# A retention layer and two expert layers on one core: 136 DMAs issued by GpSimd in place of SyncE

## The chip, the cores and the metric

The kernel runs on one core of one Trainium2 chip. A core has a matrix engine (TensorE, PE in the profile), a vector engine (VectorE, DVE), a scalar engine (ScalarE, ACT), a general engine (GpSimd, POOL), and a fifth engine, SyncE (SP), that computes nothing and issues transfers. Each engine works through its own instructions in order and waits for others on semaphores. A transfer (DMA) is an instruction of the engine that issues it: SP, ACT or POOL. The bytes are then moved by 16 DMA engines that the core shares out among all of them. An instruction behind a DMA issue that waits has to wait too, whatever it needs itself.

The metric is the time of one execution in microseconds (us). Lower is better.

## What is computed

```python
def _attn_ref(q, k, v):                                  # B, H, S, D = 4, 8, 576, 64
    scores = scale * np.matmul(q, k.transpose(0, 1, 3, 2))
    Dmat = np.where(rel >= 0, gamma[:, None, None] ** rel[None, :, :], 0.0)
    return np.matmul(scores * Dmat[None, :, :, :], v)
def _moe_ref(x, w_in, w_out):                            # 2304 x 512, 512 x 2048, 2048 x 512
    h = x @ w_in
    g = np.where(h > 0.0, h, alpha * (np.exp(np.minimum(h, 0.0)) - 1.0))
    return g @ w_out
def _moe2_ref(x, w_in, w_out):
    h = np.maximum(x @ w_in, 0.0)
    return h * h @ w_out
def reference(**kwargs):
    attn_out = _attn_ref(**attn_kwargs)
    x = np.ascontiguousarray(attn_out.transpose(0, 2, 1, 3)).reshape(B * S, H * D)
    x = _moe_ref(x=x, **moe_kwargs)
    return _moe2_ref(x=x, **moe2_kwargs)
```

Attention with a decaying mask gives 2304 tokens of width 512. Two expert layers follow: 512 to 2048 and back, the first with an exponential unit between its products, the second with a squared rectifier. The weights arrive as 64-bit floats and are turned into fp32 on the chip.

## The kernel before, in words

Every fp32 product is three matmuls of a faster type: `split` (L157 to L160) cuts an operand into a high part (ACT, L159) and the rest (DVE, L160), and `mm3` (L162 to L165) runs high by high, high by low, low by high. Products, splits and what lies between them are the whole of the work, with PE the busiest engine.

**Attention and layer one.** The 2304 tokens come in five blocks of 512, 512, 256, 512 and 512. For each block the attention runs in chunks of tokens (the q, k and v of a chunk are loaded at L256 and scaled at L267, transposed at L293, scores at L306, outputs at L321 and L325, the running state at L335 and L341). Then for each of the 16 slices f of the hidden width the kernel computes `h` (an up product over a block, lines 163 to 165), the exponential unit (ACT L365 to L367, DVE L369 and L370), and `down(blk, f)`, which adds to four PSUM accumulators `acc0` to `acc3`. Blocks 0 and 1 are shared: they go through the slices in three groups (0 to 5, 6 to 10, 11 to 15), because their accumulators are given up in between. At the end of a group `down` parks the sums in DRAM (`parts`, L406). At the end of the next group it loads them (L394) and adds them on DVE (L402), which also sets the accumulator free. After the last slice of a block the sum is layer two's input. It is stored to the DRAM tiles `x2s0` to `x2s8` in pieces of 128 x 128 (64 KB each, L411): 16 stores for a block of 512, 8 for the block of 256, 72 in all. The tiles `x2` that hold these sums are taken from the pool `raw`, three buffers that also hold raw weights and, later, layer two's inputs `r`.

**Layer two's weights** are prepared beside this. `load_raw` (L187, L192) fetches a 64-bit slice, `to_f32` (ACT L204, L205; DVE L206 to L211) turns it into fp32 in the tile `f`, of which there are three, and `park_w` (L215) stores it in the DRAM tile `w2s`: 32 stores of 256 KB. `fetch_w` (L221) reads it back later.

**Layer two** runs as a scheme of seven products for a 2 x 2 block product, products A, B and D at L492 in 128 x 384 tiles, each of six matmuls. `inputs(u)` loads `r` from `x2s[u]` (L429; 512 KB) and makes from it the operands `T` by splits (L439: ACT L159, DVE L160) and differences (L443). u runs from 0 to 8, and u = 6, 7, 8 are the third column c = 2, which need blocks 3 and 4. The sums of products become `go` (DVE L519, L522) and are stored to `g2s` (L525). The second product of layer two is at L675.

**What sets the order.** The program is written for a scheduler that decides, for each engine, the order of its instructions by modelled times; the engine of a DMA is named in the code. So a DMA on another engine moves not only itself: the rows around it may be put in another order on every engine. Before, SP issues nearly all transfers, ACT ten, and POOL none: POOL does eight scalings at the start (L267) and otherwise nothing.

The change touches `park_w` (L214, L215) and `down` (L374 to L413). Three lines of `inputs` show what has to wait for the last of the stores:

```python
def load():
    r = raw_p.tile([P, 4, 2, P], F32, tag="raw", name="r")
    nc.sync.dma_start(out=r, in_=x2s[u])
```

Of the kernel before, what the change touches and what calls it, by code (L numbers as in the profile page):

```python
# [21 lines left out]
NF = DFF // P  # L22
# [104 lines left out]
def tile_kernel(ctx: ExitStack, tc, q, k, v, w_in1, w_out1, w_in2, w_out2, cst, out):  # L127
    nc = tc.nc
# [15 lines left out]
    parts = dram.tile([2, P, KC, TB], F32, tag="parts", name="parts")  # L144
    w2s = dram.tile([2 * NF, P, DM], F32, tag="w2s", name="w2s")
# [16 lines left out]
    def mm3(ps, l_hi, l_lo, r_hi, r_lo, first, last):  # L162
        nc.tensor.matmul(ps, l_hi, r_hi, start=first, stop=False)  # L163
        nc.tensor.matmul(ps, l_hi, r_lo, start=False, stop=False)  # L164
        nc.tensor.matmul(ps, l_lo, r_hi, start=False, stop=last)  # L165


    raws, f32s, w_t = {}, {}, {}
# [43 lines left out]
        f32s[u] = a  # L212

    def park_w(u):  # L214
        nc.sync.dma_start(out=w2s[u[1] * NF + u[2]], in_=f32s.pop(u))  # L215

    def fetch_w(u, spare=None):
        a = a_p.tile([P, NP, P], F32, tag=spare, name="f") if spare else f_p.tile([P, DM], F32, tag="f", name="f")
# [155 lines left out]
    def down(blk, f):  # L374
        n = BLOCKS[blk][1]
        g, w = g_t.pop((blk, f)), w_t[0, 1, f]
        shared = blk < 2
        first, last = (any(f == r[e] - (e == 1) for r in (GROUPS if shared else ((0, NF),))) for e in range(2))
        if first:
            acc_t[blk] = [ps_acc.tile([P, TB], F32, tag="acc", name=f"acc{m}") for m in range(KC)]  # L380

        back = shared and last and f >= GROUPS[0][1]
        end = last and f == NF - 1
        part = []
        for m in range(KC if last else 0):
            if end:
                if m % 2 == 0:
                    both = raw_p.tile([P, 2, TB], F32, tag="raw", name="x2")
                t = both[:, m % 2]
            else:  # L390
                t = n_p.tile([P, TB], F32, tag="qkv"[m % 3], name="part")
            part.append(t[:, :n])
            if back:
                nc.sync.dma_start(out=part[m], in_=parts[blk, :, m, :n])  # L394
        for m in range(KC):
            c = slice(m * P, (m + 1) * P)
            a = acc_t[blk][m][:, :n]
            mm3(a, w[:, 0, c], w[:, 1, c], g[:, 0, :n], g[:, 1, :n], first, last)
            if not last:
                continue  # L400
            if back:
                nc.vector.tensor_tensor(out=part[m], in0=a, in1=part[m], op=ALU.add)  # L402
            else:
                nc.scalar.copy(part[m], a)
            if not end:
                nc.sync.dma_start(out=parts[blk, :, m, :n], in_=part[m])  # L406
                continue
            for half in range(2):
                for j in range(n // 2 // P):
                    o = half * n // 2 + j * P  # L410
                    nc.sync.dma_start(  # L411
                        out=x2s[COL0[blk] // P + j][:, m // 2 * 2 + half, m % 2], in_=part[m][:, o:o + P]
                    )  # L413

# [382 lines left out]
    for i, (blk, f) in enumerate(ORDER1):  # L797
        def mid():
            if i == SPREAD[2][0] - 4:
                load_next(True)  # L800
                load_next(True)
                scale_next()
            for of, (lo, hi) in SPREAD.items():
                if lo <= i < hi:
                    need = 3 * len(blocks[of])
                    for _ in range((i - lo + 1) * need // (hi - lo) - (i - lo) * need // (hi - lo)):
                        attn_step()
            if at["split"] < len(w1):
                w1_to(units1(i))
            elif i >= SHARED and at["f322"] < min(len(w2), units2(i)):  # L810

                step("park", at["f322"], w2, park_w)
                with tc.issue_after(mark[0]):
                    step("f322", at["raw2"], w2, to_f32)
                while at["raw2"] < min(len(w2), at["f322"] + 2):
                    step("raw2", 99, w2, lambda u: load_raw(*u))
            if at["f322"] == len(w2):
                step("park", 99, w2, park_w)
            j = i - (len(ORDER1) - NF)

            with tc.issue_after(mark[0]):
                if j == 6:
                    run(factors(0))
                if 7 <= j < NF and j not in (10, 14):
                    next_inputs()
# [3 lines left out]
        if len(pend) > LAG:  # L829
            down(*pend.pop(0))  # L830
# [25 lines left out]
    for i, (f, c) in enumerate(seq):  # L856
        now = up2(f, c)
        for n, (at_, _) in enumerate(tasks):
            if at_ == i:
                if i in (5, 18):  # L860
                    queue.extend([lambda: None] * 2)
                queue.append(lambda n=n: expand(n))
        for k in TURNS.get(i, (1, 5, 7, 2, 6, 4, 3)):
            whose = last if k in (7, 4) else now
            if whose:
                whose[k]()
            if k in (7, 4) and pend:
                down(*pend.pop(0))
            between()
        last = now  # L870

        for g in {20: (0,), 21: (1, 2), 22: (3,), 23: (4,)}.get(i, ()):
            load_last(g)
# [33 lines left out]
```

## Time and profile before

| | us |
|---|---|
| median of three runs | 889.0 (888.3 to 893.39) |
| profiled execution, its own time | 890.2 |
| span of the profiled execution | 888.4 |
| PE busy in the span | 858.9 |
| DVE busy | 685.8 |
| ACT busy | 491.9 |
| POOL busy | 8.6 |

The span is the time from the first to the last instruction that the profile holds; 1.8 us of the profiled execution's own time lie outside it. All times below that place an event (such as 526.75) are microseconds from the start of the span. PE's granted clock was 0.99 over the span, so nothing below turns on the clock. PE is busy for 97% of the span, and the rest is spread over a few stretches. What can be won or lost by transfers is therefore read from the single places where PE stands idle and from what ends each of these waits.

### The profile page before, as it was taken

The numbers are of one execution on the slowest core, as the hardware profiler recorded it, in microseconds if no ns is written. First come the engines' busy times: TensorE is split into PE (matmuls) and PEld (weight loads), VectorE is DVE, ScalarE is ACT, GpSimd is POOL, SyncE is SP. The second block draws the span as 40 slices with busy tenths as digits, with TensorE's granted clock in tenths as the row PEclk, the third lists the DMA queues.
The fourth block names the chain that finished last, engine by engine and source line by source line (L and its number), as shares of the span: only waits on it lengthen the run. The fifth ranks groups of instructions, "written<-read, shape, count | busy, mean of one in ns | idle before, by whom it ended". The sixth has DMA issues, their size and how long they took to land.

```text
span 888.4 us, 14958 instructions
## 1 busy us (share of the span) xinstructions
PE 858.9 (97%) x5630; PEld 773.1 (87%) x5630; DVE 685.8 (77%) x1391; ACT 491.9 (55%) x961; POOL 8.6 (1%) x12
## 2 busy tenths in 40 slices
PE   7798999999998999999999999999999989999998
PEld 5676888888888988888888899999989989999997
DVE  4998888885667867766779867889874769898984
ACT  3674778673464666556767754555543434444441
POOL 3000000000000000000000000000000000000000
PEclk9999899999999999999999999999999999999999
DMA  9945306383528656534362044599997993544331
GB/s 223 269 117 160 87 33 190 119 213 96 142 60 233 173 156 184 171 107 146 129 230 89 24 126 154 161 325 349 344 324 242 402 346 132 157 141 154 120 131 37
DMA packets 157608, 155.33 MB, mean 175 GB/s; under 512 B 62816, under 2 KB 121312, under 8 KB 157536
## 3 DMA queue, kind: packets, MB, share of 16 engines
q1 hardware_dynamic: 150208, 139.69, 52.0%
q10 hardware_dynamic: 7328, 14.68, 4.6%
q8 instruction: 44, 0.72, 0.4%
q14 instruction: 28, 0.23, 0.1%
HBM read 98.77 MB, written 55.57 MB: 174 GB/s over the span
## 4 chain that ended last, share of the span: by engine, by line
PE 83%; DVE 6%; DMA 5%; issue 2%; ACT 2%; SPq 1%; ACTq 0%; DVEq 0%
PE m L675 18%; PE A L492 10%; PE acc L163 7%; PE acc L164 7%; PE h L163 7%; PE acc L165 7%; PE h L164 7%; PE h L165 7%; PE D L492 5%; PE B L492 2%; PE ps_o L325 2%; PE ps_o L321 1%; PE ps_s L306 1%; DMA q<-in_q_dram 1%; DMA g<-g2s 1%
## 5 line engine op out<-in xcount | busy, mean ns | idle before, releaser
L675 PE MATMUL m<-wo,S 128*128 128x256 f32 x1512 | 184.0, 285 | 3.6 <-ACT S L159 3.6
L675 PEld LDWEIGHTS m<-wo,S 128*128 128x128 f32 x1512 | 183.3, 193 | 4.1 <-ACT S L159 4.0
L159 ACT CAST S<-g 128x512 fp32r<-128x512 f32 (+1 forms) x144 | 75.0, 567 | 95.0 <-DVE g L659 45.9
L163 PE MATMUL h<-x,w 128*128 128x512 f32 (+1 forms) x320 | 120.4, 378 | 2.2 <-DVE t L370 1.3
L164 PE MATMUL h<-x,w 128*128 128x512 f32 (+1 forms) x320 | 118.9, 372 | 0.0
L165 PE MATMUL h<-x,w 128*128 128x512 f32 (+1 forms) x320 | 118.9, 371 | 0.0
L164 PE MATMUL acc<-g,w 128*128 128x512 f32 (+1 forms) x320 | 118.5, 371 | 0.0
L165 PE MATMUL acc<-g,w 128*128 128x512 f32 (+1 forms) x320 | 117.5, 370 | 0.0
L492 PE MATMUL A<-T,pair 128*128 128x384 f32 x576 | 114.2, 339 | 1.6 <-DVE go L519 0.8
L163 PE MATMUL acc<-g,w 128*128 128x512 f32 (+1 forms) x320 | 111.4, 375 | 2.3 <-DVE x L402 1.3
L492 PEld LDWEIGHTS A<-T,pair 128*128 128x128 f32 x576 | 102.0, 190 | 3.4 <-DVE go L519 1.6
L160 DVE TENSOR_TENSOR S<-g,S 128x512 fp32r<-128x512 f32 (+1 forms) x144 | 85.9, 623 | 23.2 <-ACT S L159 21.7
L365 ACT ACTIVATE t<-h 128x512 f32<-128x512 f32 (+1 forms) x80 | 44.5, 556 | 80.5 <-PE h L165 76.9
L369 DVE SCALAR_TENSOR_TENSOR t<-e,t 128x512 f32<-128x512 f32 (+1 forms) x80 | 50.9, 636 | 46.7 <-ACT t L367 46.5
L163 PEld LDWEIGHTS h<-x,w 128*128 128x128 f32 x320 | 60.7, 190 | 14.1 <-DVE t L370 1.8
L159 ACT CAST g<-t 128x512 fp32r<-128x512 f32 (+1 forms) x80 | 46.4, 580 | 46.5 <-DVE t L370 44.7
L163 PEld LDWEIGHTS acc<-g,w 128*128 128x128 f32 x320 | 59.4, 188 | 13.4 <-DVE x L402 1.6
L165 PEld LDWEIGHTS h<-x,w 128*128 128x128 f32 x320 | 60.8, 190 | 10.7 <-DVE w L160 0.2
L164 PEld LDWEIGHTS h<-x,w 128*128 128x128 f32 x320 | 60.9, 190 | 10.2
L164 PEld LDWEIGHTS acc<-g,w 128*128 128x128 f32 x320 | 60.3, 188 | 10.2
L165 PEld LDWEIGHTS acc<-g,w 128*128 128x128 f32 x320 | 60.2, 188 | 10.1
L492 PE MATMUL D<-T,pair 128*128 128x384 f32 x288 | 58.5, 336 | 1.9 <-ACT pair L159 0.6
(88 smaller groups left out, 1282.4 us busy)
## 6 DMA issues: line engine op xcount, KB each, us to landing
g2s<-go SPq DMA_DIRECT2D x48, 384.0 KB, 4.5
g<-g2s SPq DMA_DIRECT2D x36, 512.0 KB, 3.9
raw<-in_moe_w_in_dram SPq DMA_DIRECT2D x32, 512.0 KB, 5.8
raw<-in_moe_w_out_dram SPq DMA_DIRECT2D x32, 512.0 KB, 4.8
wo2s<-wo SPq DMA_DIRECT2D x56, 256.0 KB, 4.2
wo<-wo2s ACTq DMA_DIRECT2D x9, 1536.0 KB, 14.7
w2s<-f SPq DMA_DIRECT2D x32, 256.0 KB, 2.3
f<-w2s SPq DMA_DIRECT2D x32, 256.0 KB, 4.0
```

Of the source, the lines that this page charges most:

```text
L159: nc.scalar.copy(pair_hi, src)
L160: eng.tensor_tensor(out=pair_lo, in0=src, in1=pair_hi.bitcast(F32), op=ALU.subtract)
L163: nc.tensor.matmul(ps, l_hi, r_hi, start=first, stop=False)
L164: nc.tensor.matmul(ps, l_hi, r_lo, start=False, stop=False)
L165: nc.tensor.matmul(ps, l_lo, r_hi, start=False, stop=last)
L306: nc.tensor.matmul(ps[e][:n, p, :n], kT[r, p, :n], qT[r, p, :n], start=True, stop=True)
L321: i = nc.tensor.matmul(ps[:, p, :n], st[:, p, :], qT[:, p, :n], start=p == 0, stop=True, skip_group_check=True)
L325: nc.tensor.matmul(ps[e * D:(e + 1) * D, p, :n], vn[:n, 2 * p + e, :], live[e][:n, p, :n], start=not s, stop=True, skip_group_check=True,)
L365: nc.scalar.activation(t, h, AF.Relu, scale=-1.0)
L369: nc.vector.scalar_tensor_tensor(out=t, in0=e, scalar=1.0, in1=t, op0=ALU.add, op1=ALU.mult)
L492: ins = nc.tensor.matmul(ps, w[:, l, o:o + P], t[:, r, j], start=first and i + j == 0, stop=i + j == 3, skip_group_check=True)
L675: ins = nc.tensor.matmul(m(u, k), l[:, x], w[:, y], start=first and k in (1, 6, 4, 5), stop=j == HF - 1 and i == 2, skip_group_check=True,)
```

## The change

Four lines name another engine. What is transferred, from where to where, and how it is cut, stays the same.

```diff
     def park_w(u):
-        nc.sync.dma_start(out=w2s[u[1] * NF + u[2]], in_=f32s.pop(u))
+        nc.gpsimd.dma_start(out=w2s[u[1] * NF + u[2]], in_=f32s.pop(u))
...
             if back:
-                nc.sync.dma_start(out=part[m], in_=parts[blk, :, m, :n])
+                nc.gpsimd.dma_start(out=part[m], in_=parts[blk, :, m, :n])
...
             if not end:
-                nc.sync.dma_start(out=parts[blk, :, m, :n], in_=part[m])
+                nc.gpsimd.dma_start(out=parts[blk, :, m, :n], in_=part[m])
                 continue
...
-                    nc.sync.dma_start(
+                    nc.gpsimd.dma_start(
                         out=x2s[COL0[blk] // P + j][:, m // 2 * 2 + half, m % 2], in_=part[m][:, o:o + P]
                     )
```

That is 32 stores of L215, 16 loads of L394, 16 stores of L406 and 72 stores of L411: 136 transfers that POOL issues in place of SP.

Three places show how the instructions move. A row is a line, an operation, and its tiles as out<-in with the buffer number behind the name.

SP at the start of layer two (`x2_5141` is the last half of the last block's sums; `r_5185` and `r_5296` are the inputs u = 7 and u = 8). Before:

```order
L411 DMA x2s7_102<-x2_5141 128x128
L411 DMA x2s8_103<-x2_5141 128x128
L525 DMA g2s0_104<-go_5125 128x3x256
L429 DMA r_5185<-x2s7_102 128x1024
L429 DMA r_5296<-x2s8_103 128x1024
L221 DMA f_5581<-w2s_94 128x512
L525 DMA g2s0_104<-go_5215 128x3x256
```

Of the change:

```order
L429 DMA r_5037<-x2s6_101 128x1024
L221 DMA f_5583<-w2s_94 128x512
L221 DMA f_5581<-w2s_94 128x512
L525 DMA g2s0_104<-go_5125 128x3x256
L525 DMA g2s0_104<-go_5215 128x3x256
L525 DMA g2s1_105<-go_5227 128x3x256
L525 DMA g2s1_105<-go_5293 128x3x256
L429 DMA r_5185<-x2s7_102 128x1024
L525 DMA g2s0_104<-go_5305 128x3x256
L429 DMA r_5296<-x2s8_103 128x1024
```

The stores are gone to POOL, where they are the last 16 rows. The load of `r_5185` now stands behind three more stores of `go`, the last of them `go_5293`.

DVE at the same place, where `T7` is the first operand made from `r_5185`. Before:

```order
L522 SCALAR_TENSOR_TENSOR go_5227<-go_5227 128x3x128
L160 TENSOR_TENSOR T7_5039<-r_5185,T7_5039 128x2x128
L519 TENSOR_TENSOR go_5293<-A_5187,m5_5205 128x3x128
L160 TENSOR_TENSOR T7_5039<-r_5185,T7_5039 128x2x128
L443 TENSOR_TENSOR r_5185<-r_5185 128x256
L160 TENSOR_TENSOR T8_5044<-r_5185,T8_5044 128x2x128
L522 SCALAR_TENSOR_TENSOR go_5293<-go_5293 128x3x128
L519 TENSOR_TENSOR go_5305<-B_5298,c1_5272 128x3x128
```

Of the change:

```order
L519 TENSOR_TENSOR go_5293<-A_5187,m5_5205 128x3x128
L522 SCALAR_TENSOR_TENSOR go_5293<-go_5293 128x3x128
L519 TENSOR_TENSOR go_5305<-B_5298,c1_5272 128x3x128
L522 SCALAR_TENSOR_TENSOR go_5305<-go_5305 128x3x128
L519 TENSOR_TENSOR go_5305<-D_5276,u2_5316 128x3x128
L522 SCALAR_TENSOR_TENSOR go_5305<-go_5305 128x3x128
L519 TENSOR_TENSOR go_5371<-A_5265,m5_5283 128x3x128
L522 SCALAR_TENSOR_TENSOR go_5371<-go_5371 128x3x128
L519 TENSOR_TENSOR go_5383<-B_5376,c1_5350 128x3x128
L160 TENSOR_TENSOR T7_5039<-r_5185,T7_5039 128x2x128
L522 SCALAR_TENSOR_TENSOR go_5383<-go_5383 128x3x128
L160 TENSOR_TENSOR T7_5039<-r_5185,T7_5039 128x2x128
```

The first `T7` stands nine rows later: the sums `go_5293`, `go_5305`, `go_5371` and the first piece of `go_5383` go ahead of it.

PE at the end of the last group of block 1 (`acc2_2522` is an accumulator that DVE has to empty at L402, with the parked sum `x2_2420`, before PE may write to it again). The difference, with + for rows that the change puts there:

```order
 L165 MATMUL h_2723<-x_2019,w3_706 128x256
+L163 MATMUL h_2723<-x_2019,w3_706 128x256
...
+L321 MATMUL ps_o_2665<-qT_2560,st_109 128x128 x4
+L325 MATMUL ps_o_2665<-P0_2624,v_2262 64x128
...
+L335 MATMUL ps_u_2680<-v_2262,k_2260 64x64 x8
+L163 MATMUL h_2782<-x_2019,w4_922 128x256
...
+L293 MATMUL ps_t_2742<-cs_108,q_2500 128x128 x4
+L293 MATMUL ps_t_2749<-cs_108,k_2502 128x128 x4
 L163 MATMUL acc2_2522<-g_2329,w0_210 128x256
```

The rest of one `h` product (3 matmuls), the attention outputs `ps_o` (4 and 8), the state `ps_u` (8), a whole `h` product (12) and eight transposes now come before the first write to `acc2_2522`; before, they came behind it.

## Rows read from the trace of the kernel before

**Rows 1.** The page, section 1: engines, busy us (share of the span), instructions

```profile
PE 858.9 (97%) x5630; PEld 773.1 (87%) x5630; DVE 685.8 (77%) x1391; ACT 491.9 (55%) x961; POOL 8.6 (1%) x12
```

**Rows 2.** Stretches of 50 us: length, busy us of each engine, granted clock, DMA

```profile
150.00:200.00 50.00, 50.00 (x235) 41.13 (x235) 42.09 (x75) 35.92 (x63) 0.00 (x0) 1.00 0.60 163
...
250.00:300.00 50.00, 46.93 (x444) 43.83 (x444) 36.52 (x78) 27.26 (x62) 0.00 (x0) 1.00 0.66 174
300.00:350.00 50.00, 49.57 (x393) 43.03 (x392) 38.59 (x80) 32.63 (x69) 0.00 (x0) 1.00 0.54 149
...
500.00:550.00 50.00, 48.53 (x255) 44.73 (x254) 36.46 (x85) 27.08 (x63) 0.00 (x0) 1.00 0.35 108
550.00:600.00 50.00, 49.67 (x287) 49.33 (x286) 39.90 (x85) 27.90 (x58) 0.00 (x0) 1.00 0.72 234
```

**Rows 3.** Timeline of PE, 262 to 283: start, us, what, [idle before <-releaser]

```profile
270.74 0.39 PE L163 MATMUL acc<-g,w 128*128 128x256 f32 x1 [1.26 <-DVE x L402]
...
280.40 0.66 PE L293 MATMUL ps_t<-cs,q 128*128 128x128 f32 x4 [1.19 <-DVE x L160]
```

**Rows 4.** Timeline of SP's DMA issues, 225 to 300: start, us, what, how many

```profile
260.33 4.05 SPq L411 DMA_DIRECT2D x2s<-x  x8
...
270.71 4.91 SPq L411 DMA_DIRECT2D x2s<-x  x8
```

**Rows 5.** Chain of work that ended last, 255 to 283: start, us, what

```profile
265.69 1.85 DMA x<-parts
...
269.99 0.70 DVE x L402
...
271.12 0.12 PE acc L164
...
273.40 0.89 PE ps_o L321 x8
...
275.73 3.30 DMA q<-in_q_dram
```

**Rows 6.** Transfers: what, issuer, count, KB each, median us from issue to landing

```profile
x<-parts SPq DMA_DIRECT2D x8, 256.0 KB, 3.8
```

**Rows 7.** Chain of work that ended last, 515 to 548

```profile
525.06 1.67 DMA x2s<-x
...
526.75 4.86 DMA r<-x2s
...
532.07 0.43 DVE T L160
```

**Rows 8.** Timeline of SP's DMA issues, 500 to 560

```profile
517.60 8.37 SPq L411 DMA_DIRECT2D x2s<-x  x16
```

**Rows 9.** Timeline of PE, 530 to 566

```profile
533.02 1.32 PE L492 MATMUL A<-T,pair 128*128 128x384 f32 x6 [0.44 <-DVE go L519]
...
538.34 1.20 PE L492 MATMUL B<-T,pair 128*128 128x384 f32 x6
...
540.98 1.32 PE L492 MATMUL A<-T,pair 128*128 128x384 f32 x6 [0.39 <-DVE go L519]
...
544.23 0.34 PE L492 MATMUL D<-T,pair 128*128 128x384 f32 x1
545.21 1.15 PE L492 MATMUL D<-T,pair 128*128 128x384 f32 x5 [0.64 <-DVE T L160]
```

**Rows 10.** Timeline of DVE, 530 to 546

```profile
538.69 1.43 DVE L160 TENSOR_TENSOR T<-r,T 128x256 fp32r<-128x256 f32 x4
540.03 0.42 DVE L443 TENSOR_TENSOR r<-r 128x256 f32<-128x256 f32 x1
```

**Rows 11.** Line 411's instructions on SP: duration ns min/median/max, first and last start

```profile
L411 SPq DMA_DIRECT2D x2s<-x x72: 319/430/1814, 226.5 to 525.5; - x72
```

**Rows 12.** Groups of POOL's instructions: busy us, mean ns of one, idle before

```profile
L267 POOL TENSOR_TENSOR spare<-spare,cs 128x512 f32<-128x512 f32 x6 | 6.3, 1049 | 8.7 <-DMA spare<-in_q_dram 7.0 <-DMA spare<-in_k_dram 1.5
```

**Rows 13.** Line 206's instructions: duration ns min/median/max, first and last start

```profile
L206 DVE TENSOR_SCALAR f<-f x64: 409/420/828, 14.3 to 455.3; 128x512 f32<-128x512 f32 x64
```

## The prediction

> **What bounds the kernel now.** The page's section on engines comes first: PE is busy for 97% of the span, POOL for 1% [rows 1]. A PE that is nearly full can win little, so the next view is the table of busy time in stretches of 50 us, which says where the missing 3% lies. In the stretches that the change touches PE is full for 50.00 of 50 us where the parks and the partial sums of the first two groups are moved (150 to 200), and it loses 3.07 us in 250 to 300, 0.43 in 300 to 350, 1.47 in 500 to 550 and 0.33 in 550 to 600 [rows 2]. These 5.3 us are all that a better order of transfers could give back there. PE's own timeline then gives each idle place with what ended it: 1.26 us at 270.74 for the addition of a parked sum, 1.19 at 280.40 for a split of an attention input [rows 3], and 0.44, 0.39 and 0.64 at 533.02, 540.98 and 545.21 for sums and operands of layer two [rows 9]. Last, the chain of waits and SP's timeline tell what stands behind each.
>
> At 270.74 it is DVE's addition at 269.99, behind a load of the parked sum that SP issues only at 265.69 [rows 5], after SP has spent 260.33 to 264.38 on eight stores of L411 [rows 4]. At 280.40 it is the load of q at 275.73, which begins when SP has ended the next eight stores, 270.71 to 275.62 [rows 4, 5]. At 533 it is SP again: 16 stores from 517.60 on take 8.37 us [rows 8], the landing of the fifteenth (the last that u = 7 needs) ends at 526.73, the load of r takes 4.86, and after a cast on ACT, DVE starts on it at 532.07 [rows 7]. So SP, full of small stores, is late three times, and the change takes these stores from it. What has to be priced is POOL as their issuer.
>
> **The price of one issue on POOL.** POOL issues no transfer in the trace of before, so this price, c, has to be bounded. SP's own median for a store of L411 is 0.43 us, its longest 1.81 [rows 11]. POOL's only regular work, a 128 x 512 operation, takes 1.05 us [rows 12]. Nothing excludes either end. I take c = 1.04, near that row, since it is the one row that shows how fast POOL gets through an instruction, and keep 0.43 and 1.81 as ends. The Trainium skill, "DMA: Bandwidth & Descriptors" (Latency and other measured facts), gives a first byte after some 1 us for a transfer from GpSimd and 0.6 from SP; no run here shows it yet, and by it the load of r below would come 0.4 us later and the sum would be 889.8.
>
> **Parts that cost nothing.** The 32 parks (L215) and the parked sums of the first groups lie where PE is 50.00 of 50 us busy [rows 2]: no engine waits for a park before layer two fetches it much later, and 32 x 1.04 = 33 us of POOL stand against hundreds of idle ones [rows 1]. The cover is POOL's idleness; it is gone only where POOL has a row of stores with a consumer behind it, which are the two places below.
>
> **Layer one, 256 to 335.** Removed are both waits behind SP. The load of q no longer queues behind eight stores (minus 1.19). For the parked sum, POOL's order is: two loads of the first half, one park, eight stores of L411, then the two loads of the second half. The first store begins at 260.4 as before [rows 4]. The load is issued after eight stores, takes c to issue, lands 3.4 later (3.8 from issue to landing [rows 6], less 0.43 of issue), and DVE adds in 0.70 [rows 5]: 260.4 + 9c + 4.1, that is 273.9 at c = 1.04, against 270.69 before. So the sum itself gets later. But PE would have had nothing to do from 270.74 - 1.26 = 269.48 on, and now has the work that the order moved ahead: ps_o and ps_u (273.40 to 275.73, 2.33), 15 products of h at 0.12 (1.8) and two groups of transposes at 0.66 (1.32) [rows 3, 5]. That is 5.45 us, to 274.9. No stall up to c = 1.16, so minus 1.26. Beyond it PE waits 9 us for each us of c. This stretch: -2.45.
>
> **Start of layer two, 517 to 548.** POOL's first store starts at 517.6. The fifteenth is issued at 517.6 + 15c; it lands 1.24 after that (1.67 less 0.43), and r takes 4.86 [rows 7]: r is there at 523.7 + 15c, 539.3 for c = 1.04 against 531.6 before. SP's queue adds nothing to that: the load stands behind the store of go_5293, a sum that reads a product already done when PE comes to wait at 533.02 [rows 9], and at c = 1.04 the stores are done later, at 534.5. The new order on DVE expects this and puts go_5293 to go_5383 ahead of the first T7. go_5383 reads the product that PE runs from 538.34 for 1.20 us [rows 9]; with PE's 0.44 of waiting before it taken off it ends at 539.1, and DVE is through its addition at 539.6. So T7 begins at 539.6 or at r's landing + 0.46 (531.61 to 532.07 [rows 7]), which is 539.8 at c = 1.04. From there to the T9 that PE needs stand 20 rows of splits and differences, 0.335 each (538.69 to 540.03 for four [rows 10]), and three rows of sums at 0.55: 8.35 us, to 548.1. PE, without its waits, would be at that product's wait at 544.23 + 0.34 - 0.44 - 0.39 = 543.7 [rows 9]. It waits 4.4 us where it waited 1.47: +2.9. At c = 0.43 the order alone sets it: 547.95, +2.7. Beyond c = 1.03 each us of c costs 15.
>
> **The sum.** -2.45 + 2.9 = +0.4 or so against the profiled execution's 890.2, so 890.6 there; that execution lies 1.2 above the median of the runs, 889.0, and the forecast on that scale is 889.4. At c = 0.43 it is -2.45 + 2.7, 889.3. At c = 1.16 it is +2.3, 891.3; at c = 1.25 layer two +6.1, layer one's stall +0.8 and the -2.45 give 893.4. At c = 1.81: layer two +14.5, layer one 260.4 + 16.3 + 4.1 - 274.9 = +5.9, with the -2.45 it is +18, 907.
>
> **Rivals.** (1) *Slower: POOL's row of 16 stores becomes the chain.* Place: the last block's stores before r is loaded. Price: 24 us for each us of c above 1.16 (15 in layer two and 9 in layer one). It reaches 1% (8.9 us, about what a measurement of this kernel can tell from no change) at c = 1.44. For it: SP itself had stores of 1.81 [rows 11]; against it: the only POOL row is at 1.05 [rows 12]. Between 1.16 and 1.44 it gives 891.3 to 898, above 898 to 907.
>
> (2) *Descriptors that wait for DVE.* The row: L206, one input of 512 columns, takes 0.42 us on DVE, while the addition of two inputs takes 0.70 [rows 5, 13]; these fast passes run until 455.3, so only the layer-one stores meet them. If each of the nine issues there waits for one such pass, the parked sum is ready 9 x 0.42 = 3.8 us later, at 277.7; PE waits 2.8, and the time is 892.2. Layer two's stores, after 517, meet none. This is what the Trainium skill, "SBUF — State Buffer" (SBUF: two separate sides), says of transfers issued from GpSimd: their descriptors can't be written while DVE runs in a mode that takes the port both share, and it advises SP or ACT as issuer, which speaks against this change; no trace here shows it so far.
>
> (3) *Faster: all waits go.* If the new order also closes the small gaps (all of the 5.3 us of [rows 2], and r comes early enough), it is 884. Against it: nine rows were put ahead of T7, so DVE can't be earlier than 539.6 there. A gain over 1% isn't in these stretches at all.
>
> (4) *Nothing happens*: the waits are given back at once by other work, and layer two hides r: 889.0. It can't be told from my forecast by the time, but by PE's idle places.
>
> **Chances.** Forecast (c up to 1.16, 889.3 to 891.3) 0.50; (4) 0.07; (2) 0.09; (1) with c from 1.16 to 1.44, 0.12, above that 0.16; (3) 0.04; a gain over 1% from what I have not seen 0.02. Within 1% are the first four and (3): 0.82; slower 0.16; faster 0.02. The range reaches from 885.5, just above (3), to 899, which takes in (2), the middle of (1) and the first of what lies above it; without it are 0.14 of rival (1), 0.04 and 0.02. The forecast's own range is 888.3 to 891.3, from the lowest run of before to c = 1.16.
>
> **What would show it.** In the changed kernel's profile: the duration of L411 on POOL's queue is c, and should be about 1.04. PE shows no idle place for L402 near 270 nor for the split of q near 280; if L402 is there, c is above 1.16 or descriptors waited. r lands near 539 and not 531.6; PE waits some 4 us for a T or a go between 540 and 549. SP's L411 rows are gone and its L256 rows near 264 to 270 come early. The forecast is wrong if a store takes over 1.2 us on POOL, if the loads on SP turn out to wait for something other than SP's queue, or if PE waits in a stretch that is full today.

## The result and the profile after

The changed kernel takes 901.2 us (median of five runs, 898.4 to 906.2) against 889.4 of the kernel before in the same set; the ratio, estimated over the runs of both, is 1.0123, 95% interval 1.0093 to 1.0153. A second set gave 899.2 against 889.3, 1.0106 (1.0077 to 1.0135). It is slower by about 1.1%, and it lies above the range of the forecast, which ended at 899. (One more execution, the first that was profiled, took 2155 us, with PE busy 2.5 times as long for the same matmuls; it is left out, and all rows below are of a second profile, whose execution took 899.24.)

The head of the page of the changed kernel: span, and busy time by engine.

```profile
span 897.5 us, 15045 instructions
...
PE 862.4 (96%) x5630; PEld 774.6 (86%) x5630; DVE 687.0 (77%) x1391; ACT 490.6 (55%) x961; POOL 82.9 (9%) x148
```

The span grew by 9.1 us, from 888.4 to 897.5, and PE's busy time by 3.5 [rows 1]. POOL's 136 issues are its 74 us more. So PE both waits longer and works longer on the same 5630 matmuls. The stretches of 50 us show where (columns as in [rows 2]: length, busy PE, PEld, DVE, ACT, POOL, then the granted clock):

```profile
250.00:300.00 50.00, 46.24 (x437) 42.60 (x438) 36.57 (x78) 25.19 (x59) 14.03 (x26) 1.00 0.55 149
...
500.00:550.00 50.00, 47.30 (x243) 42.94 (x241) 35.26 (x80) 27.48 (x65) 8.56 (x16) 1.00 0.36 115
550.00:600.00 50.00, 46.48 (x254) 45.91 (x254) 36.78 (x80) 25.01 (x52) 0.00 (x0) 0.93 0.53 173
```

In 250 to 300 PE loses 3.76 us (3.07 before). In 500 to 550 it loses 2.70 (1.47 before), and in 550 to 600 3.52 (0.33 before), with a granted clock of 0.93 where it was 1.00.

The two profiled executions lie 9.0 us apart (899.2 and 890.2). To see where these go I matched the same matmul (the n-th of its line and tile) in both traces and took the difference of its starts. The changed kernel lies behind the one before by

| at (time of before) | behind, us | step |
|---|---|---|
| 190 | 0.8 | start of the kernel, where executions of one kernel differ by as much |
| 230 to 255 | 2.5 | +1.7, from 195 to 225: block 1's parked sums at the end of the second group |
| 355 to 510 | 3.8 | +1.3, layer one's last work on block 1, 260 to 350 |
| 551 to 600 | 10.4 | +6.6, start of layer two, 533 to 551 |
| 665 to the end | 9.0 | -1.4, layer two's later waits |

The forecast had 0, -2.45 and +2.7 (at POOL's real price) for the middle three (195 to 225, 260 to 350, start of layer two).

**Start of layer two.** PE's timeline of the changed kernel, with its waits:

```profile
544.53 1.21 PE L492 MATMUL D<-T,pair 128*128 128x384 f32 x6
547.77 0.44 PE L492 MATMUL A<-T,pair 128*128 128x384 f32 x1 [2.04 <-ACT T L159]
548.88 1.15 PE L492 MATMUL A<-T,pair 128*128 128x384 f32 x5 [0.66 <-DVE T L160]
553.22 2.46 PE L492 MATMUL D<-T,pair 128*128 128x384 f32 x6 [3.19 <-ACT T L159]
```

The waits are 2.04 + 0.66 + 3.19 = 5.9 us; before, they were 0.44 + 0.39 + 0.64 [rows 9]. The last row also takes 2.46 us for six matmuls that take 1.21 in the first. The granted clock (last but two column) tells why:

```profile
551.00:554.00 3.00, 0.78 (x2) 0.58 (x3) 2.46 (x8) 1.42 (x4) 0.00 (x0) 0.51 0.00 0
554.00:557.00 3.00, 3.00 (x10) 3.00 (x10) 0.33 (x1) 0.48 (x1) 0.00 (x0) 0.50 0.02 5
557.00:560.00 3.00, 3.00 (x16) 3.00 (x16) 2.21 (x4) 0.09 (x1) 0.00 (x0) 0.85 0.00 0
```

Between 551 and 557 it is 0.50 to 0.51 of the full speed: PE is at the lower of its two levels, 1.2 GHz, from within the third of these waits on. Busy time in these nine microseconds, weighed by the clock that is missing, is 0.78 x 0.49 + 3.0 x 0.50 + 3.0 x 0.15 = 2.3 us lost. So the 6.6 us are 4.4 more of waiting and 2.2 to 2.3 of clock.

**Parked sums at the end of the second group.** Two additions hold PE for 0.31 and 0.62 us, where the kernel before had one wait of 0.24, at 220.23:

```profile
198.76 0.50 PE L163 MATMUL acc<-g,w 128*128 128x512 f32 x1 [0.31 <-DVE part L402]
222.73 0.50 PE L163 MATMUL acc<-g,w 128*128 128x512 f32 x1 [0.62 <-DVE part L402]
```

What these waits have more than before is under half of the 1.7 us; the rest of the step is not explained here.

**Layer one.** PE's timeline near the last parked sum of block 1:

```profile
279.93 1.16 PE L306 MATMUL ps_s<-qT,kT 64*128 64x128 f32 x16 [1.09 <-ACT kT L298]
283.04 0.39 PE L163 MATMUL acc<-g,w 128*128 128x256 f32 x1 [1.94 <-DVE x L402]
```

Waits of 1.09 and 1.94 us, so the addition at L402 still holds PE, at 283.04 where it did at 270.74 [rows 3].

### The profile page after: what moved, and what is told of

Its sections match the earlier page's. It is cut to its first block, busy times and chain, and to the rows that moved or that the text cites. A ratio compares the mean times of both kernels' runs of the same rounds, so it can differ in the third digit from the quotient of the medians.

```text
span 2153.6 us, 15045 instructions
## 1 busy us (share of the span) xinstructions
PE 2138.1 (99%) x5630; PEld 1614.5 (75%) x5630; DVE 696.7 (32%) x1391; ACT 494.0 (23%) x961; POOL 82.5 (4%) x148
## 3 DMA queue, kind: packets, MB, share of 16 engines
q0 software_dynamic: 7424, 21.50, 2.9%
## 4 chain that ended last, share of the span: by engine, by line
PE 99%; DVE 1%; ACT 0%; issue 0%; DVEq 0%
PE m L675 21%; PE A L492 12%; PE h L163 8%; PE acc L164 8%; PE h L165 8%; PE acc L163 8%; PE acc L165 8%; PE h L164 8%; PE D L492 6%; PE B L492 3%; PE ps_s L306 2%; PE ps_o L325 2%; PE ps_t L293 2%; PE ps_o L321 2%; PE ps_u L335 1%; PE warm L712 0%
## 5 line engine op out<-in xcount | busy, mean ns | idle before, releaser
L675 PEld LDWEIGHTS m<-wo,S 128*128 128x128 f32 x1512 | 450.8, 441 | 0.0
L675 PE MATMUL m<-wo,S 128*128 128x256 f32 x1512 | 450.6, 529 | 0.0
L492 PE MATMUL A<-T,pair 128*128 128x384 f32 x576 | 274.2, 680 | 1.3 <-DVE T L160 1.3
L163 PE MATMUL h<-x,w 128*128 128x512 f32 (+1 forms) x320 | 247.4, 774 | 0.1
L165 PE MATMUL h<-x,w 128*128 128x512 f32 (+1 forms) x320 | 247.2, 773 | 0.0
L164 PE MATMUL acc<-g,w 128*128 128x512 f32 (+1 forms) x320 | 245.9, 768 | 0.0
L492 PEld LDWEIGHTS A<-T,pair 128*128 128x128 f32 x576 | 202.0, 353 | 57.9 <-issue 50.4
L164 PE MATMUL h<-x,w 128*128 128x512 f32 (+1 forms) x320 | 245.0, 765 | 0.0
L165 PE MATMUL acc<-g,w 128*128 128x512 f32 (+1 forms) x320 | 244.1, 766 | 0.0
L163 PE MATMUL acc<-g,w 128*128 128x512 f32 (+1 forms) x320 | 232.7, 775 | 0.0
L165 PEld LDWEIGHTS h<-x,w 128*128 128x128 f32 x320 | 118.8, 371 | 63.5 <-issue 63.1
L163 PEld LDWEIGHTS h<-x,w 128*128 128x128 f32 x320 | 117.5, 368 | 59.7 <-issue 53.8
L164 PEld LDWEIGHTS acc<-g,w 128*128 128x128 f32 x320 | 117.9, 369 | 59.0 <-issue 56.6
L164 PEld LDWEIGHTS h<-x,w 128*128 128x128 f32 x320 | 117.3, 366 | 58.9 <-issue 58.8
L165 PEld LDWEIGHTS acc<-g,w 128*128 128x128 f32 x320 | 116.7, 365 | 57.5 <-issue 56.7
L163 PEld LDWEIGHTS acc<-g,w 128*128 128x128 f32 x320 | 112.4, 357 | 62.4 <-issue 58.7
L492 PE MATMUL D<-T,pair 128*128 128x384 f32 x288 | 139.9, 683 | 2.7 <-ACT T L159 2.0
L159 ACT CAST S<-g 128x512 fp32r<-128x512 f32 (+1 forms) x144 | 75.0, 564 | 282.9 <-PE m L675 135.4
L492 PEld LDWEIGHTS D<-T,pair 128*128 128x128 f32 x288 | 100.5, 352 | 31.5 <-issue 24.0
```

Of the source, the lines that this page charges most:

```text
L159: nc.scalar.copy(pair_hi, src)
L492: ins = nc.tensor.matmul(ps, w[:, l, o:o + P], t[:, r, j], start=first and i + j == 0, stop=i + j == 3, skip_group_check=True)
L675: ins = nc.tensor.matmul(m(u, k), l[:, x], w[:, y], start=first and k in (1, 6, 4, 5), stop=j == HF - 1 and i == 2, skip_group_check=True,)
```

## The experiments

Each kernel was timed beside the kernel before, in 4 to 12 runs. "Change" is the changed kernel. Times of different sets are compared by their ratios, and each trace is of one execution.

| kernel | us | ratio to before (95%) |
|---|---|---|
| change, again | 899.2 | 1.0106 (1.0077 to 1.0135) |
| only L411 on POOL | 898.5 | 1.0092 (1.0061 to 1.0122) |
| only L394 and L406 on POOL | 892.8 | 1.0032 (1.0004 to 1.0059) |
| only L215 on POOL | 890.7 | 1.0006 (0.9989 to 1.0024) |
| change, last block's L411 on SP | 896.9 | 1.0072 (1.0044 to 1.0099) |
| change, go's stores pinned | 899.8 | 1.0126 (1.0074 to 1.0178) |
| change, r for u = 7, 8 on POOL | 899.7 | 1.0115 (1.0076 to 1.0154) |
| before, L411 joined in pairs, on SP | 891.3 | 1.0012 (0.9987 to 1.0038) |
| before, last block's L411 on POOL | 897.0 | 1.0081 (1.0050 to 1.0112) |
| L215 and L411 but the last block's on POOL | 892.0 | 1.0019 (1.0001 to 1.0038) |
| change, last block on SP, raw loads on POOL | 889.6 | 1.0001 (0.9977 to 1.0026) |
| raw loads, L215, L411 but the last block's on POOL | 892.6 | 1.0028 (1.0009 to 1.0048) |
| before, raw loads on POOL | 891.2 | 1.0022 (1.0005 to 1.0038) |
| before, raw loads and L215 on POOL | 890.0 | 1.0009 (0.9990 to 1.0028) |

### The change again, and its lines one by one

> The changed kernel once more, for a profile at full speed. POOL issues a store in 0.54 us in the first profile, so the price that the prediction left open sits near its lower end, and the prediction's own sum gives 889.3. Theory 1 (new waits of PE): the 12 us stand as idle places of PE, in layer one near 230 to 340 or at the start of layer two near 517 to 560, and PE's busy time is 859 as before. Theory 2 (clock): the granted clock was 0.980 to 0.987 in the fast executions against 0.99, so PE works for some stretch at the lower of its two levels after a wait; PE's busy time is then 4 to 8 us above 858.9 and the idle places hold only the rest. Theory 3 (no single place): the losses are spread in pieces under 1 us. Expected time 899 to 903.

Both the waits and the clock are there, as shown above. The price that the forecast left open, the issue of a store on POOL (duration in ns, min/median/max):

```profile
L411 POOL DMA_DIRECT2D x2s<-x x72: 537/538/647, 229.3 to 530.7; - x72
```

0.54 us, near the lower end of the bounds (0.43 to 1.81) and half of the 1.04 that I took.

```diff
-                    nc.sync.dma_start(      # L411 alone
+                    nc.gpsimd.dma_start(
```

> Only the 72 stores of layer two's input (L411) are issued by POOL. If the loss comes from the start of layer two, where DVE's order puts nine rows ahead of the first T7, this one has nearly all of it: 898 to 902. If it comes from the parks or the parked sums: 886 to 890.

898.5: the stores of L411 alone make nearly the whole loss. Matched in the same way, its trace (of an execution of 901.4) loses 6.2 us at the start of layer two and 4.3 in layer one.

```diff
-                nc.sync.dma_start(out=part[m], in_=parts[blk, :, m, :n])      # L394 and L406 alone
+                nc.gpsimd.dma_start(out=part[m], in_=parts[blk, :, m, :n])
...
-                nc.sync.dma_start(out=parts[blk, :, m, :n], in_=part[m])
+                nc.gpsimd.dma_start(out=parts[blk, :, m, :n], in_=part[m])
```

> Only the stores and loads of the parked sums (L394, L406) are issued by POOL. If the loss is at the start of layer two: 887 to 890. If the loads of parked sums land later from POOL, or the new order around the end of a group costs PE: 892 to 902, with an idle place of PE that ends with L402.

892.8, at the low end of the second expectation, and an idle place of PE ends with L402 as it said (0.62 us at 222.12). Its trace loses 1.7 us between 195 and 225, as the change does, and gains 1.0 between 260 and 340. The parked sums cost something by themselves.

```diff
-        nc.sync.dma_start(out=w2s[u[1] * NF + u[2]], in_=f32s.pop(u))      # L215 alone
+        nc.gpsimd.dma_start(out=w2s[u[1] * NF + u[2]], in_=f32s.pop(u))
```

> Only the 32 parks of layer two's weights (L215) are issued by POOL. Nobody waits for a park, so 887 to 890 by every theory but one: if descriptors written by GpSimd are held up by DVE, a park holds its tile f longer, to_f32 comes later, and the time is over 892.

890.7, no difference by the interval. The parks were free, as forecast.

### One place: the last block's 16 stores

```diff
-                    nc.sync.dma_start(      # in the kernel before
+                    (nc.gpsimd if blk == 4 else nc.sync).dma_start(
```

> The kernel before with only the last block's 16 stores (L411) issued by POOL; PE's order is the same as before throughout, and DVE's, ACT's and SP's order differs only at the start of layer two, as in the change. If that place costs what the changed kernel's trace shows there (4.4 us of waits and 2.2 us at the lower clock level), the time is 895 to 897, with PE waiting about 6 us between 540 and 552. If its loss needs the rest of the change, 889 to 891.

897.0, as expected: 16 stores, with the rest of the kernel before and PE's order unchanged, cost 6.9 us, and its trace has all 6.9 at this place. PE's waits in this kernel, and two stretches with the granted clock:

```profile
542.72 0.68 PE L492 MATMUL A<-T,pair 128*128 128x384 f32 x1 [2.24 <-ACT T L159]
543.81 1.97 PE L492 MATMUL A<-T,pair 128*128 128x384 f32 x5 [0.41 <-DVE T L160]
548.16 2.46 PE L492 MATMUL D<-T,pair 128*128 128x384 f32 x6 [2.38 <-ACT T L159]
```

```profile
540.00:550.00 10.00, 4.97 (x14) 3.54 (x13) 8.69 (x24) 5.55 (x16) 0.00 (x0) 0.64 0.27 91
550.00:560.00 10.00, 10.00 (x51) 9.99 (x51) 4.37 (x8) 2.46 (x5) 0.00 (x0) 0.85 0.20 67
```

2.24 + 0.41 + 2.38 = 5.0 us of waits, and the clock goes to 0.64 and 0.85. The counter-test, with these 16 stores alone back on SP:

```diff
-                    nc.gpsimd.dma_start(      # in the changed kernel
+                    (nc.sync if blk == 4 else nc.gpsimd).dma_start(
```

> The changed kernel, but the last block's 16 stores (L411) stay on SP; DVE's order at the start of layer two is then that of before. Theory 1 (the start of layer two holds most of the loss: 4.4 us more idle time of PE and 2.2 us at the lower clock level right behind it): PE's waits there are again about 1.5 us, the granted clock stays at 1.00, and the time falls by 6 to 7 us against the changed kernel, to 892 to 894. Theory 2 (the loss sits in layer one): it stays at 898 to 901.

The waits at this place are back to what they were before,

```profile
546.60 1.33 PE L492 MATMUL A<-T,pair 128*128 128x384 f32 x6 [0.38 <-DVE go L519]
...
550.83 1.14 PE L492 MATMUL D<-T,pair 128*128 128x384 f32 x5 [0.64 <-DVE T L160]
```

and in its trace the start of layer two costs nothing (-0.4 us). But the time fell only to 896.9, not to 892 to 894: this trace lost 3.9 us in layer one, where that of the change lost 1.3. The waits there are 1.52 and 1.92 us, and the clock fell behind them:

```profile
280.00:285.00 5.00, 3.08 (x25) 2.89 (x26) 4.01 (x7) 0.79 (x2) 1.72 (x4) 0.64 0.30 73
285.00:290.00 5.00, 5.00 (x41) 4.71 (x40) 2.22 (x6) 3.10 (x9) 0.95 (x2) 0.67 0.67 222
```

In the profile of the change, waits of 1.09 and 1.94 us had left it at 1.00. Up to the start of layer two four of the profiled kernels have the same rows in the same order on every engine: the change, this one, and the two of the next section. In layer one their waits at this place sum to 3.0 us (change), 3.4 (last block on SP), 2.5 (go's stores pinned) and 3.4 (r on POOL), and they lose 1.3, 3.9, 0.6 and 4.3 us. The clock stayed at 1.00 in the first and the third and fell in the other two, in the last to

```profile
285.00:290.00 5.00, 5.00 (x25) 4.78 (x26) 3.51 (x8) 3.38 (x8) 2.35 (x5) 0.50 0.63 213
```

So waits that differ by some 0.3 us ended at either level, and the same order costs 0.6 to 4.3 us here. The 1.3 us of the change's trace is one of these four. That the clock here also makes the spread of its runs (898.4 to 906.2) is likely but not shown, as the others were not profiled.

### What holds T at the start of layer two

In the changed kernel the load of r for u = 7 was issued at 539.10, seen in SP's timeline, while POOL had issued its last store by 531.25:

```profile
525.69 13.19 SPq L525 DMA_DIRECT2D g2s<-go  x4
539.10 0.33 SPq L429 DMA_DIRECT2D r<-x2s  x1
```

```profile
521.79 7.66 POOL L411 DMA_DIRECT2D x2s<-x  x14 [58.84 <-ACT x L404]
530.11 1.14 POOL L411 DMA_DIRECT2D x2s<-x  x2 [0.66 <-issue]
```

It stood behind a store of go (L525) that waited for ACT's L571, the second half of the sum. DVE's first T then began at 544.52:

```profile
542.70 0.56 DVE L519 TENSOR_TENSOR go<-B,c 128x384 f32<-128x384 f32 x1
544.52 0.43 DVE L160 TENSOR_TENSOR T<-r,T 128x256 fp32r<-128x256 f32 x1 [1.26 <-ACT T L159]
```

Two things could hold T: SP's queue, or DVE's own order. Two kernels take the first away.

```diff
-            nc.sync.dma_start(out=r, in_=x2s[u])
+            (nc.gpsimd if u >= 7 else nc.sync).dma_start(out=r, in_=x2s[u])
```

> The changed kernel, but the loads of r for u = 7 and 8 are issued by POOL, behind its own stores, so no store of go stands ahead of them. DVE's order is that of the changed kernel: T7 behind go_5383. Theory SP queue alone: r lands near 537, PE's waits fall to 2 us, 893 to 895. Theory both (SP's queue and DVE's order hold T7 about equally late: go_5383 is ready at 543.3, T7 began at 544.5): T7 begins at 543.3, PE's waits fall only by 1 to 2 us, 896 to 900.

899.7: no clear gain in time. r is loaded by POOL at 537.18, and it lands 4.7 to 5.1 us later, at 542:

```profile
537.18 0.55 POOL L429 DMA_DIRECT2D r<-x2s  x1 [1.68 <-DMA x2s<-x]
```

```profile
DMA to landing us min/median/max: 4.7/4.9/5.1
```

DVE's first T begins at 547.25, with no wait ahead of it, right behind the sum go_5383 that the order puts there:

```profile
546.78 0.56 DVE L519 TENSOR_TENSOR go<-B,c 128x384 f32<-128x384 f32 x1
547.25 0.42 DVE L160 TENSOR_TENSOR T<-r,T 128x256 fp32r<-128x256 f32 x1
```

T begins 0.47 us after the start of that row, where it was 1.82 in the change. PE waits 1.31 and 3.20 us:

```profile
551.12 1.69 PE L492 MATMUL A<-T,pair 128*128 128x384 f32 x6 [1.31 <-ACT T L159]
556.01 2.46 PE L492 MATMUL D<-T,pair 128*128 128x384 f32 x6 [3.20 <-ACT T L159]
```

So r was there for five microseconds before DVE, in its fixed order, came to it. This is what the theory "both" expected: T is 1.4 us earlier, PE waits 1.4 us less (4.5 in place of 5.9), and the time stays in 896 to 900. By the matched starts this trace loses 5.1 us at the start of layer two in place of 6.6, and layer one's 4.3 hide that gain. The second kernel pins the stores of go:

```diff
-            nc.sync.dma_start(
+            tc.keep_in_program_order(nc.sync.dma_start(
                 out=g2s[c][:, f, :, h].rearrange("s p h c -> p s (h c)"),
```

> All four lines on POOL as in the change, but the stores of go (L525) are kept in program order on SP, so that the load of r for u = 7 stands ahead of the stores of go_5215, go_5227 and go_5293, and DVE's T7 ahead of go_5371. Theory SP queue (r was loaded at 539.1, 6 us after its stores had landed, because it stood behind a store of go that waited for ACT L571): r is loaded near 533, PE's waits at 545 to 553 shrink from 5.9 to 2 us or less, the clock does not fall, 893 to 895. Theory POOL (the stores issued by POOL land late): r is loaded no earlier than 538 and the time stays at 898 to 901.

899.8, though r was loaded at 529.28 (it lands by 535, since no load of r took over 5.7 us in this run) and T7 stood ahead of go_5371:

```profile
529.28 0.32 SPq L429 DMA_DIRECT2D r<-x2s  x1
```

PE waits 4.13 us:

```profile
548.32 2.46 PE L492 MATMUL D<-T,pair 128*128 128x384 f32 x6 [4.13 <-ACT T L159]
```

ACT makes the first half of T (the cast at L159) only at 537.91, behind a copy (L509) that waits for a product of PE:

```profile
537.53 0.48 ACT L509 COPY m<-D 128x384 f32<-128x384 f32 x1 [0.56 <-PE D L492]
537.91 1.02 ACT L159 CAST T<-r 128x256 fp32r<-128x256 f32 x3
```

DVE's first T follows at 538.35, and sums of go, the last of them from a product that PE runs later, still stand ahead of its last T. In both kernels the expectation that SP's queue alone was the cause fell: with r there early, PE waits 4.1 to 4.5 us all the same, and in the first, where PE, ACT and DVE keep the order of the change, the queue is worth 1.4 of the 5.9 us. What is left goes by the orders of ACT and DVE, as fixed before the kernel runs. (The second kernel's trace loses 4.1 us here and 2.1 more up to 665, where its order differs again.) One test was not made: the stores on POOL with these two orders as in the kernel before.

### What holds PE in layer one

The q that PE waited for in the kernel before, issued there at 275.73 [rows 5], is issued 28 us earlier in the changed kernel. The next q was issued at 273.36, and SP's waits in 225 to 300 say why (total, times, longest):

```profile
247.97 0.37 SPq L256 DMA_DIRECT2D q<-in_q_dram  x1
...
260.85 0.72 SPq L256 DMA_DIRECT2D v<-in_v_dram  x1
272.22 1.03 SPq L187 DMA_DIRECT2D raw<-in_moe_w_in_dram  x2
273.36 0.61 SPq L256 DMA_DIRECT2D q<-in_q_dram  x1
```

```profile
SPq L256 <- PE ps_u L335: 25.3, 4, 12.0
SPq L187 <- DVE f L211: 22.6, 3, 10.5
```

From 261.6 to 272.2 SP stood in a raw load (L187) of layer two's weights, whose tile DVE was still converting; q and k were behind it. In the chain of work this q, 7.72 us from issue to landing, is what the last addition waits for, since DVE scales q (L267) ahead of it:

```profile
273.36 7.72 DMA q<-in_q_dram
...
282.38 0.61 DVE x L402
```

```profile
281.09 0.68 DVE L267 TENSOR_TENSOR q<-q,cs 64x512 f32<-64x512 f32 x1 [1.22 <-DMA q<-in_q_dram]
```

The kernel before issued this q still later, and it cost nothing, because there the last addition (the second of these rows) did not stand behind it:

```profile
278.83 0.62 SPq L256 DMA_DIRECT2D q<-in_q_dram  x1
```

```profile
271.20 0.69 DVE L402 TENSOR_TENSOR x<-acc,x 128x512 f32<-128x512 f32 x1
```

So it takes both, DVE's new order and the q behind the raw load. The same raw load, landing late, also makes the other wait, of 1.09 us: ACT converts it ahead of the copy kT that PE needs:

```profile
277.68 0.69 ACT L204 ACTIVATE raw<-raw 128x512 int32<-128x512 uint32 x1 [2.80 <-DMA raw<-in_moe_w_in_dram]
```

```diff
         if which == 0:
-            i = nc.sync.dma_start(
+            i = (nc.sync if layer == 0 else nc.gpsimd).dma_start(      # and the same in the other branch (L192)
```

This edit on top of the kernel with the last block on SP:

> The changed kernel with the last block's stores on SP, and the raw loads of layer two's weights (L187, L192) issued by POOL too, so that no q, k or v load on SP stands behind a raw load that waits for DVE's conversion. If this wait is what makes q late at 281 in the changed kernel (q issued at 273.4, SP in a raw load's wait since 261.6), PE's waits between 265 and 285 fall by 3 us or more and the time is 890 to 893, against 896.9 with the raw loads on SP. If another wait holds q or the parked sum just as long, 895 to 898.

889.6, some 6 us below the kernel without this edit by the ratios (1.0001 and 1.0072). The q load starts at 262.03, and PE is busy for 49.17 of 50 us in 250 to 300, where it was 46.24 in the change; against the kernel without this edit the waits in 265 to 285 fall by 3.4 us, as expected, and the clock stays at 1.00:

```profile
262.03 0.62 SPq L256 DMA_DIRECT2D q<-in_q_dram  x1
```

```profile
250.00:300.00 50.00, 49.17 (x490) 46.31 (x489) 39.83 (x88) 29.68 (x68) 18.95 (x32) 1.00 0.62 165
```

The raw load as the cause is thus borne out, but the edit also changed DVE's and PE's order, so it is not shown by itself. Next, with the parked sums on SP, without and with the raw loads on POOL:

> POOL issues the parks (L215) and the stores of L411 of all blocks but the last; the parked sums (L394, L406) and the last block's stores stay on SP. If the 1.7 us that the change loses between 195 and 225 are due to the parked sums' place on POOL, this kernel has lost nothing by 230. If in 250 to 350 the q loads still stand behind a raw load (L187) that waits for its tile, it loses 2 to 5 us there and gives 891 to 894; if the parked sums were the cause there too, 886 to 889.

892.0, in the first range. Nothing is lost between 195 and 225, so the 1.7 us there come with the parked sums on POOL. PE loses 2.0 us in 290 to 300 instead.

> Parks, raw loads of layer two's weights and L411 of all blocks but the last on POOL; parked sums and the last block's stores on SP. It joins the two former edits. If both causes are right and add up, nothing is lost by 230, PE's waits in 250 to 350 are below the 3.5 us of before, and the time is 885 to 888, better than both kernels; if they don't add up, 889 to 893.

892.6: the edits don't add up; this order waits 2.63 us up to 284.98. And the raw loads without the change's lines:

> The kernel before with only the raw loads of layer two's weights (L187, L192) issued by POOL; parks, parked sums and all stores of L411 stay on SP. If q's lateness in 250 to 350 comes from raw loads on SP that wait for their tile, PE's waits there (3.5 us before) fall below 2 us and the time is 885 to 888. If it comes from the rows of L411 on SP, as my prediction had it, nothing changes there: 888 to 891.

891.2, above both ranges (1.0005 to 1.0038): no gain. The raw loads on SP were not the only cause. With the parks:

> As raw_only, with the parks (L215) on POOL as well: SP then has in 250 to 350 only q, k, v, the parked sums and the stores of L411, and what waits for DVE's conversions is all on POOL. If the two waits add up, 884 to 887; if PE's waits there are set by something else, 888 to 891.

890.0, no difference either. What SP has to be rid of is settled only in part: the change alone loses here (1.3 us in its trace), the raw loads' move alone loses (1.4), and together, with the last block on SP, they gain (2.9). No version here is measurably faster than the kernel before.

### Fewer stores on SP

```diff
+                    boths.append(both)
...
+            if m % 2 == 0:
+                continue
...
                     nc.sync.dma_start(
-                        out=x2s[COL0[blk] // P + j][:, m // 2 * 2 + half, m % 2], in_=part[m][:, o:o + P]
+                        out=x2s[COL0[blk] // P + j][:, m // 2 * 2 + half], in_=boths[m // 2][:, :, o:o + P]
                     )
```

> The kernel before, all on SP, with pairs of neighbouring stores of L411 joined: 36 stores of 128 KB instead of 72 of 64 KB. If SP's row of small stores is what makes r and q late, SP is through 3 to 4 us earlier at the end of each block and the waits of PE at 270, 280 and 533 to 545 (3.9 us) go in part: 885 to 888. If the second half of a pair waits for the first and eats that up: 888 to 891.

891.3, above both ranges, and no difference by the interval. The last block's stores take SP 5.29 us instead of 8.37, and of the three waits at the start of layer two one of 0.68 us is left, but the time is not better.

## Why the prediction was wrong

**POOL's price (1.04, range 0.43 to 1.81).** Mis-sized: 0.54. It was not the term that decided: with 0.54 the same sum gives 889.3.

**The rival that was to make it slower.** It didn't: POOL's 16 stores were issued by 531.25 and r could have been loaded some six microseconds before it was. The clock and the new waits in layer one, which did make it slower, were not among the rivals.

**Start of layer two (+2.7).** The mechanism of the wait was right and was in the rows of the order: T7 stands behind go_5383, and "the order alone sets it". The size failed: the place cost 6.6 us. The first part is the wait, +4.4 instead of +2.7. I had T7 at 539.6, 543.4 on the changed trace's time (3.8 later), and it began at 544.52: "SP's queue adds nothing" is wrong by 1.1 us. I looked at DVE's half of go_5293 and not at ACT's (L570, L571), for which the store also waits. From T7 to the product D I had 8.35 us, and it took 8.70. I also had PE wait only at D, from 547.5 on, and it stood from 545.73 on, at the A product ahead of it; but that is mostly the same wait at an earlier row and adds only some 0.2. The second part was put at nothing: I priced a wait of PE at its length, on the premise that nothing turns on the clock. That holds for the kernel before; in the changed kernel the clock took 2.3 us more. The kernel with only these 16 stores on POOL shows this place by itself: 6.9 us.

**Layer one (-2.45).** Wrong in sign: +1.3 in the change's trace, 0.6 to 4.3 in the four traces with these rows. The term of 1.19 came true: the q that waited behind eight stores came 28 us earlier. The step that failed is "No stall up to c = 1.16", where I had the last addition follow the load of its parked sum, at 268.7 by my sum for c = 0.54. The first store began at 263.79 and not at 260.4, and the load, behind eight stores and a wait for DVE, at 268.73. The additions began at 276.40 and 282.30, the last one behind the next q, and that q stood on SP behind a raw load that waits for its tile. PE waits 1.94 us for it, more than the 1.26 that were to go. I had read one wait ahead of each transfer and not what stands ahead of the additions in the new order.

**Parts that cost nothing.** Right for the parks (1.0006). Wrong for block 1's parked sums at the end of the second group, 195 to 225, where two additions hold PE and the trace loses 1.7 us. I had taken the stretch 150 to 200 as cover and not looked at 200 to 225, where the trace of before already has a wait for L402.

**The signs.** Two of the three signs of being wrong came true: a load on SP waited for its tile and not for SP's queue, and PE waits in a stretch that was full (0.31 us at 198.76). Another sign misled: L402 still holds PE, and yet c was 0.54, and no issue on POOL took over 0.72 us in that trace.

**The other rivals.** Descriptors that wait for DVE would have shown as a longer issue or landing. Landing times of the changed kernel (median us):

```profile
w2s<-f POOLq DMA_DIRECT2D x32, 256.0 KB, 4.4
...
x2s<-x POOLq DMA_DIRECT2D x72, 64.0 KB, 2.1
```

A park lands in 4.4 us instead of 2.3, a store of L411 in 2.1 instead of 1.7. The parks lie among DVE's fast passes, so the trace agrees in direction with the Trainium skill, "SBUF — State Buffer" (SBUF: two separate sides), but nobody waits for a park, and no run here separates that cause. With the raw loads on POOL too, parks from POOL land in 2.4 to 3.4 us, so the issuer alone does not set the 4.4. The Trainium skill, "DMA: Bandwidth & Descriptors" (Issuing engine by pattern), names Sync for simple loads and stores; the 0.43 us of an issue on SP against 0.54 on POOL point the same way, though this is not what made the change slower.

The chance for slower was 0.16, tied to a price of 1.44 and more. What the chances lacked is a case of its own for a new order that costs more than the waits it takes away.

## What to carry to other kernels

When a transfer changes its queue, price the order before the issue: read what now stands ahead of the late operand on the engine that uses it, and what waits in the old queue behind the transfers that left. On an in-order queue a wait that is taken away can uncover the next one. And a wait of PE can cost more than its length: here the clock fell behind some waits of 3 to 6 us and not behind others.

## What was not expected of the hardware

A store of 64 KB and one of 256 KB take POOL the same time to issue, 0.54 us each. The page counts POOL's 136 transfers (21.50 MB) as a queue of its own kind, software_dynamic, and SP's as hardware_dynamic. PE's granted clock fell to 0.50 within the waits of 2.04, 0.66 and 3.19 us at the start of layer two and stayed there up to 557. In layer one, with the same rows, it stayed at 1.00 behind waits of 1.09 and 1.94 us and fell to 0.64 behind 1.52 and 1.92.
